# Transposing the global rows' probabilities of the last two batches by DMA instead of on TensorE

## The chip, the core and the metric

The kernel runs on one core of one Trainium2 chip. The metric is device microseconds (us) of one execution; lower is better. The kernel before took 308.22 us, the median of three runs that lie between 307.31 and 308.99.

## The reference

Block-sparse attention (4 batches, 8 heads, 768 positions, head size 64) is followed by a two-layer network on its output. Positions are grouped in 24 blocks of 32. A query block sees its neighbours, the first and the last block, and three sampled blocks. Queries of the first and the last block see all 768 keys; these are the *global rows* that the change is about.

```python
scores = scale * q @ k.T                       # per batch and head, 768 x 768
mask = (|blk_i - blk_j| <= 1) | blk_i in (0, 23) | blk_j in (0, 23) | sampled
attn = softmax(where(mask, scores, -1e9))      # over the keys
x = (attn @ v)                                 # -> 3072 tokens x 512
h = x @ w_in                                   # 512 -> 2048
out = (h * sigmoid(beta * h)) @ w_out          # 2048 -> 512, float32
```

## The kernel before

**Attention, ordinary rows.** Each batch has 11 *pairs* of query blocks, 44 in all, numbered n. For pair n, `kg` and `kn` on POOL (or DVE) collect its 8 key blocks per query block into KG, SP's DMAs `vg` fetch the value rows into VG (from pair 6 on three buffers in turn: a load for pair n waits for `av` of pair n - 3), `sc` on PE makes the scores, `mx` on DVE the row maxima, `ex` on ACT the exponentials PP, `rc` and `nrm` scale them, `tp` on PE transposes them, `ptv` on DVE or ACT moves the transposed tile to PT, `av` on PE multiplies with VG, and `xv` moves the result to xT. The sampled value rows are one DMA of 32 KB each, six for a pair, beside one or three larger ones; `vv` (L663) loads the block numbers of two pairs into SP's registers.

**Attention, global rows.** Each batch has four *units* w of 128 rows (4 heads x 32 queries) by 768 keys; over the batches they are numbered m = 0 to 15. `gs` (L911, PE) makes the scores of two units at once in four PSUM banks. Then for each unit: `gm` (L925, L927, DVE) the negated maximum; `ge` (L932, ACT) two exponentials of 384 columns into PG[m % 2]; `gr` (L939, L940, DVE) the reciprocal of the sum; `gn` (L943, POOL) scales PG; `gt` (L951, PE) six 128x128 transposes into one PSUM bank; `gptv` (L953, DVE) copies that bank into PTG. When all four units of a batch are in PTG, `gav` (L965, PE) multiplies with V and `gx` moves the result to xT. PG has two buffers, so `ge` of unit m waits for `gt` of unit m - 2. PTG has one, so `gptv` of a batch waits for `gav` of the batch before.

**The key order.** Key s stands in row p, step j of the value tile, with s = 6 p + j. So transpose j takes every sixth column of PG, from column j on.

**The network.** Tokens go through in eight groups G of 8 or 16 blocks: `h` (L1027, PE), `tanh` (L1033, ACT), `stt` (L1038, DVE), `y` (L1054, PE), `oe` (L316, ACT) and `od` (L1072 to L1075, SP's DMA to the output). A group needs the xT of its blocks; the last two groups, 6 and 7, hold batch 3 alone. The global blocks of a batch belong to its last group.

**Order.** Nothing is scheduled on the chip. A planner in the kernel (class `Plan`) runs a list scheduling in Python: every task has an engine or a choice of engines, a booked duration, a priority `prio` plus a hand-set `OFFSET`, its dependencies, and the PSUM banks that it opens and closes. DMA tasks on SP or ACT also carry `dma` (booked transfer time) and `hw` (DMAs that they issue). The planner's order of tasks is the order in which instructions are written; each engine then runs its own in that order and waits where a dependency is not met. Units of batch b carry the priorities `10.0 * ((5, 11.5, 18, 31)[b] + 0.5 * w) + 5`, where pair n carries 10 n.

Of the kernel before, what the change touches and what calls it, by code (L numbers as in the profile page):

```python
# [36 lines left out]
class Plan:  # L37
# [21 lines left out]
    def add(self, *a, **k):  # L59
        t = Task(*a, **k)  # L60
        self.tasks.append(t)
        return t
# [154 lines left out]
def kernel(  # L217
# [11 lines left out]
    nc = tc.nc  # L229

    B, H, S, D = q.shape
    BLK = 32
    NB = S // BLK
    P = 128
    J = S // P
# [24 lines left out]
    NLATE, PTA, ODS, AHEAD = 11, 1.0, 0.8, 3  # L260
    NHOT, NV = 0, 2
    NHL, UP = 4, 1024.0
    WIDE = 16

    SR, SG0, SN, SG1 = 0, 3, 4, 7
# [23 lines left out]
    PTG = sb("PTG", [P, J, 4, P])  # L289
# [14 lines left out]
    add = plan.add  # L304
    bank = lambda name: banks[plan.bank[name]]
# [26 lines left out]
    def emit_warm():  # L332
# [3 lines left out]
        out=warm[:, 0:1], in_=warm[:, 1:2], func=AF.Exp), deps=[t_warm0], prio=-150)  # L336
# [53 lines left out]
    for part, f in enumerate((emit_mask0, emit_mask1, emit_mask2)):  # L390
# [4 lines left out]
        deps=[t_mrow], prio=-90, lat=0.2, opens=("mask",))  # L395
    t_mask = add("maskc", "DVE", 0.2, lambda: nc.vector.tensor_copy(
        out=maskr[:, :, :].rearrange("x a b -> x (a b)"), in_=bank("mask")[:, 0:NM]),
        deps=[t_mb], prio=-66, closes=("mask",))
# [13 lines left out]
    pj = sb("pj", [P, J], FP32)  # L412
    mi32 = sb("mi32", [1, BLK], I32)

    def emit_selc():
# [8 lines left out]
        out=srow, in_=sf[:, 0:2 * NSEL, :].rearrange("o a r -> o (a r)")), deps=[t_idx], prio=-98)  # L424
    t_selw = []
    for f in range(2):
        def emit_sb(f=f):
# [9 lines left out]
            out=sel16[:, f * SH:(f + 1) * SH], in_=bank(("selb", f))[:, 0:SH]),  # L437
            deps=[tb], prio=-88, closes=(("selb", f),)))
    t_sel = [add(f"sel16.{j}", "DVE", 0.27, lambda j=j: nc.vector.tensor_scalar(
        out=sel[j], in0=sel16, scalar1=pj[:, j:j + 1], scalar2=None, op0=ALU.is_equal),  # L440
        deps=t_selw, prio=-66.2) for j in range(J)]
# [5 lines left out]
        out=beta_row, in_=moe_beta.rearrange("(q x) -> q x", q=FQ)), prio=-140, dma=0.1, hw=1)  # L447
    t_id32 = add("id32", "DVE", 0.2, lambda: nc.vector.tensor_copy(
        out=ident32, in_=identity[0:4, 0:4]), deps=[t_ident], prio=-64)

    def emit_betaT():
        for i in range(4):
# [3 lines left out]
                  deps=[t_beta0, t_id32], prio=-55, lat=0.2, opens=("beta",))  # L456
    t_beta = add("betah", "DVE", 0.2, lambda: nc.vector.tensor_scalar(
        out=beta_sb[:, :].rearrange("x (q i) -> x i q", i=4),
        in0=bank("beta")[:, 0:N_FFC].rearrange("x (i q) -> x i q", i=4),
        scalar1=0.5, scalar2=None, op0=ALU.mult),  # L460
        deps=[t_betaT], prio=-55, closes=("beta",))
# [20 lines left out]
    for z, (i, nm, t, dst) in enumerate(((2, "V", v, None), (0, "K", k, RK), (1, "Q", q, RQ))):  # L482
        for f in range(2):
            tl = add(f"ld{nm}0.{f}", "SP", 0.47, lambda i=i, t=t, f=f: nc.sync.dma_start(
                out=stage_half(i, f) if i < 2 else v_stage[:, f * HH:(f + 1) * HH, :],
                in_=src6(t, 0, f * HH, HH)), prio=-80 + z * 2 + f, dma=2.0 if z + f else 3.4, hw=1)
# [4 lines left out]
            for hp in range(2 * f, 2 * f + 2):  # L491
# [3 lines left out]
                        out=dst[:, 2 * hp:2 * hp + 2, :], in_=stage32(i, hp)),  # L495
                    deps=[tl], prio=-72 + 4 * i + hp)
# [3 lines left out]
        out=(w_in_sb[0:1, 0, 0:1], w_in_sb[0:1, 0, 2 * FQ * P:2 * FQ * P + 1], w_out_sb[0:1, 0, 0:1])[i],  # L500
        in_=vgate(n)), prio=-57.5 + i, deps=[ld0["Q", 1]] if n < 0 else [])
# [8 lines left out]
    for fq in range(4):  # L510
        fs = slice(fq * FQ * P, (fq + 1) * FQ * P)
        for c in range(0, 4, 2):
            t_win.append(add(f"win{fq}.{c // 2}", "POOL", 0.6, lambda c=c, fs=fs: nc.gpsimd.dma_start(
                out=w_in_sb[:, c:c + 2, fs], in_=w_in_r[:, c:c + 2, fs]),
                deps=[touch[fq // 2]], prio=-50 + 0.2 * fq + 0.05 * c, dma=1.3, bulk=THR))
    for c in range(4):
        for f in range(2):
            ps = slice(64 * f, 64 * f + 64)
            t_wout.append(add(f"wout{c}.{f}", "POOL", 0.6, lambda c=c, ps=ps: nc.gpsimd.dma_start(
                out=w_out_sb[ps, 4 * c:4 * c + 4, :].rearrange("x i m -> x (i m)"), in_=w_out_r[c, ps, :]),  # L520
                deps=[touch[2]], prio=-49 + 0.2 * c + 0.1 * f, dma=1.3, bulk=THR))
# [7 lines left out]
    for b in range(B):  # L529
        pr = prep_prio(b)  # L530
# [369 lines left out]
    for b in range(B):  # L900
        for w, (blk, u) in enumerate((bl, u) for bl in (NB - 1, 0) for u in range(2)):
            pr = 10.0 * ((5, 11.5, 18, 31)[b] + 0.5 * w) + 5
            m, s_ = gun, SG[gun % 2]
            pg = PG[gun % 2]

            def emit_gs(b=b, blk=blk, m=m):
                for hf in range(2):
                    for hp in range(NHP):
                        for uu in range(2):
                            rows = slice(uu * D, (uu + 1) * D)  # L910
                            nc.tensor.matmul(  # L911
                                bank(("GS", m + uu, hf))[hp * BLK:(hp + 1) * BLK, 0:S // 2],
                                lhsT=QT[b % 2][rows, hp, blk * BLK:(blk + 1) * BLK],
                                rhs=KT[b % 2][rows, hp, hf * (S // 2):(hf + 1) * (S // 2)],
                                start=True, stop=True, skip_group_check=True,
                                tile_position=(uu * D, hp * BLK))
            if u == 0:
                gs = add(f"gs{m}", "PE", 0.34, emit_gs, deps=([mx[GSB + w, 1]] if b == 0 else []) + [evK[b, hp] for hp in range(NHP)] +
                         [evQ[b, hp] for hp in range(NHP)], prio=pr, lat=0.2,
                         opens=tuple(("GS", m + uu, hf) for uu in range(2) for hf in range(2)))  # L920
                gsc_all.setdefault(b, []).append(gs)

            def emit_gm(m=m, s_=s_):
                for hf in range(2):
                    nc.vector.tensor_reduce(out=s_[:, hf:hf + 1], in_=bank(("GS", m, hf))[:, 0:S // 2],  # L925
                                            axis=AX.X, op=ALU.max, negate=True)
                nc.vector.tensor_reduce(out=s_[:, 2:3], in_=s_[:, 0:2], axis=AX.X, op=ALU.min)  # L927
            gm = add(f"gm{m}", "DVE", 1.15, emit_gm, deps=[gs] + ([gn[m - 2]] if m >= 2 else []), prio=pr)

            def emit_ge(m=m, s_=s_, pg=pg):  # L930
                for hf in range(2):
                    nc.scalar.activation(  # L932
                        out=pg[:, hf * (S // 2):(hf + 1) * (S // 2)], in_=bank(("GS", m, hf))[:, 0:S // 2],
                        func=AF.Exp, bias=s_[:, 2:3], scale=1.0, accum_out=s_[:, 3 + hf:4 + hf])
            ge = add(f"ge{m}", "ACT", 1.12, emit_ge, deps=[gm] + ([gt[m - 2]] if m >= 2 else []), prio=pr,
                     closes=(("GS", m, 0), ("GS", m, 1)))

            def emit_gr(s_=s_):
                nc.vector.tensor_reduce(out=s_[:, 5:6], in_=s_[:, 3:5], axis=AX.X, op=ALU.add)  # L939
                nc.vector.reciprocal(out=s_[:, 6:7], in_=s_[:, 5:6])  # L940
            gr = add(f"gr{m}", "DVE", 0.26, emit_gr, deps=[ge], prio=pr)
            gn[m] = add(f"gn{m}", {"POOL": 0.9, "DVE": 0.44}, None, lambda eng, s_=s_, pg=pg: (
                nc.vector if eng == "DVE" else nc.gpsimd).tensor_scalar(  # L943
                out=pg, in0=pg, scalar1=s_[:, 6:7], scalar2=1.0, op0=ALU.mult, op1=ALU.mult),
                deps=[gr], prio=pr)

            def emit_gt(m=m, pg=pg):
                o = bank16(("GT", m))
                pj = pg[:, :].rearrange("x (p j) -> x j p", j=J)
                for j in range(J):  # L950
                    nc.tensor.transpose(out=o[:, j * P:(j + 1) * P], in_=pj[:, j, :], identity=identity)  # L951
            gt[m] = add(f"gt{m}", "PE", 0.34, emit_gt, deps=[gn[m]], prio=pr, lat=0.2, opens=(("GT", m),))
            gptv[m] = add(f"gptv{m}", "DVE", 0.47, lambda m=m, w=w: nc.vector.tensor_copy(  # L953
                out=PTG[:, :, w, :],
                in_=bank16(("GT", m))[:, 0:J * P].rearrange("x (j m) -> x j m", j=J)),
                deps=[gt[m]] + ([gavt[b - 1]] if b else []), prio=pr, closes=(("GT", m),))
            gun += 1

        def emit_gav(b=b):
            o = bank(("GO", b))  # L960
            for hp in range(NHP):
                for j in range(J):
                    for u in range(2):

                        nc.tensor.matmul(  # L965
                            o[u * D:(u + 1) * D, hp * 2 * BLK:(hp + 1) * 2 * BLK],
                            lhsT=Vn[b % 2][:, j, (2 * hp + u) * D:(2 * hp + u + 1) * D],
                            rhs=PTG[:, j, u::2, hp * BLK:(hp + 1) * BLK],
                            start=(hp + j == 0), stop=(j == J - 1), skip_group_check=True,
                            tile_position=(0, u * D))  # L970
        gavt[b] = add(f"gav{b}", "PE", 0.75, emit_gav, deps=[gptv[gun - 4 + w] for w in range(4)] +
                      vperm[b], prio=pr, lat=0.2, opens=(("GO", b),))
        def emit_gx(eng, b=b):
            c0 = x_of(b * NB + NB - 1)
            copy_on(eng, xT[:, :, c0:c0 + 2 * BLK],
                    bank(("GO", b))[:, 0:2 * NHP * BLK].rearrange("x (h m) -> x h m", h=NHP))
        evs = [add(f"gx{b}", {"DVE": 0.42, "ACT": 0.38}, None, emit_gx, deps=[gavt[b]], prio=pr,
                   closes=(("GO", b),))]
        for blk in (0, NB - 1):
            xw[b * NB + blk] = evs  # L980
# [133 lines left out]
```

## Time and profile before

| | |
|---|---|
| median of three runs | 308.22 us |
| the profiled execution, its own time | 306.66 us |
| its span, first to last instruction | 304.9 us |
| granted TensorE clock, mean | 0.994 |
| L951 `gt`, 96 transposes on PE | 216 / 219 / 260 ns each (min, median, max) |
| L953 `gptv`, 16 copies on DVE | 536 / 548 / 557 ns each |
| L932 `ge`, 32 exponentials on ACT | 569 / 580 / 630 ns each |
| L943 `gn`, 16 scalings on POOL | 894 / 902 / 904 ns each |
| `gav` of batches 0, 1, 2, 3 starts at | 78.5, 107.8, 160.2, 215.0 us |
| last `av` (pair 43) starts at | 263.9 us |

All times in a trace are us from the start of the span. A matmul's duration overlaps with that of the next one, so PE's work is read from how far the starts lie apart, not from the sum of durations. The execution's own time is 1.8 us longer than its span. "SPq" is SP's queue of DMA issues, which the page does not count as busy time. Loads of K, Q and V of the next batch run on POOL's own DMA queue.

### The profile page before, as it was taken

To read this page: it belongs to the slowest core of one execution; us is meant where nothing else is said; L and a number is where in the kernel's file an instruction comes from. 1 tells how busy PE (TensorE), PEld (TensorE's weight loads), DVE (VectorE), ACT (ScalarE), POOL (GpSimd) and SP (SyncE) were. 2 spreads that over 40 slices of the span, in tenths; PEclk is the share of its full clock that TensorE was granted. 3 is DMA by queue.
4 is the path that set the end of the run, shared out by engine and by line. 5 is a ranking of instruction groups with operands and counts; after the bars stand their busy time and mean duration, and the time that the engine had idled before them with its cause. 6 is when DMAs were issued, how large, how long until landed. Compare 5 with 4: busy or idle time off the path is not lost.

```text
span 304.9 us, 11891 instructions
## 1 busy us (share of the span) xinstructions
PE 284.7 (93%) x4209; PEld 177.3 (58%) x4209; DVE 241.3 (79%) x562; ACT 219.8 (72%) x639; POOL 172.9 (57%) x513
## 2 busy tenths in 40 slices
PE   2699869999999899999998999999999999999994
PEld 0455658657855785665556555556555555554671
DVE  4857989999999999999999579989789765780260
ACT  3347669889788999898759599978689837771461
POOL 3079895044689678899784486868646942100000
PEclk9999979999999999999999999999999999999999
DMA  7999999978999462479943633234343242101202
GB/s 254 370 295 207 233 208 231 221 219 136 165 208 183 119 190 74 123 145 166 210 124 116 203 123 97 73 85 124 100 155 106 75 121 90 37 0 57 83 1 69
DMA packets 43445, 44.17 MB, mean 145 GB/s; under 512 B 6005, under 2 KB 39414, under 8 KB 43386
## 3 DMA queue, kind: packets, MB, share of 16 engines
q1 hardware_dynamic: 31056, 32.13, 35.1%
q0 software_dynamic: 12320, 11.27, 24.8%
q8 instruction: 33, 0.54, 0.7%
q14 instruction: 26, 0.21, 0.2%
q10 hardware_dynamic: 10, 0.01, 0.0%
HBM read 45.23 MB, written 9.44 MB: 179 GB/s over the span
## 4 chain that ended last, share of the span: by engine, by line
PE 70%; DVE 18%; DMA 6%; issue 2%; ACT 2%; SPq 1%; POOL 0%; DVEq 0%
PE bank L1027 26%; PE bank L1054 20%; PE bank L821 5%; DMA VG<-VT 4%; DVE ST L776 4%; PE bank L848 4%; PE bank L560 3%; PE bank L729 3%; DVE SG L925 3%; DVE VG L312 3%; DMA g<-in_k_dram 3%; PE bank L753 2%; PE bank L763 2%; PE bank L856 2%; DVE PTG L953 2%
## 5 line engine op out<-in xcount | busy, mean ns | idle before, releaser
L784 ACT ACTIVATE PP<-bank,ST 128x256 f16<-128x256 f32 x176 | 81.4, 479 | 20.6 <-DVE ST L776 12.4
L1027 PE MATMUL bank<-xT,w_in_sb 128*128 128x256 f16 (+1 forms) x512 | 94.0, 328 | 1.4 <-DVE g L1038 0.9
L1054 PE MATMUL bank<-w_out_sb,g 128*128 128x512 f16 x384 | 92.3, 380 | 0.0
L1038 DVE SCALAR_TENSOR_TENSOR g<-t,bank 128x512 f16<-128x512 f16 (+1 forms) x128 | 66.5, 546 | 19.4 <-ACT t L1033 19.0
L1033 ACT ACTIVATE t<-bank,beta_sb 128x512 f16<-128x512 f32 (+1 forms) x128 | 70.4, 594 | 13.5 <-PE bank L1027 9.6
L807 POOL TENSOR_SCALAR PP<-PP,ST 128x256 f16<-128x256 f16 x132 | 63.4, 497 | 27.6 <-DVE ST L801 27.6
L634 POOL COPY KG<-KT 128x64 f32 x264 | 52.0, 247 | 32.4 <-PE bank L763 18.8
L1027 PEld LDWEIGHTS <-w_in_sb 128*128 128x128 f16 x512 | 53.7, 115 | 25.8 <-issue 4.6
L776 DVE TENSOR_REDUCE ST<-bank 128x2 f32<-128x512 f32 x88 | 57.4, 680 | 3.4 <-PE bank L763 2.1
L1054 PEld LDWEIGHTS <-g 128*128 128x128 f16 x384 | 34.4, 98 | 38.2 <-issue 4.9
L784 ACT ACTIVATION_READ_ACCUMULATOR PP<-bank,ST 128x1 f32 x176 | 37.0, 210 | 0.0
L316 ACT ACTIVATE osb<-bank 128x512 f32<-128x512 f32 x24 | 14.5, 605 | 19.6 <-PE bank L1054 19.5
L312 DVE COPY PT<-bank 128x1024 f16<-128x1024 f16 x39 | 26.7, 685 | 2.4 <-PE bank L821 1.6
L821 PE MATMUL bank<-identity,PP 128*128 128x128 f16 x352 | 28.0, 224 | 0.3 <-ACT PP L784 0.3
L943 POOL TENSOR_SCALAR PG<-PG,SG 128x768 f16<-128x768 f16 x16 | 14.4, 900 | 23.9 <-ACT PG L932 19.8
L821 PEld LDWEIGHTS <-PP 128*128 128x128 f16 x352 | 22.8, 100 | 7.6 <-issue 1.3
L312 DVE CAST xT<-bank 64x256 f16<-64x256 f32 (+1 forms) x33 | 13.9, 420 | 8.4 <-ACT xT L310 7.4
L848 PEld LDWEIGHTS <-VG 128*128 128x128 f16 x448 | 16.5, 98 | 6.7 <-DMA VG<-VT 1.0
L932 ACT ACTIVATE PG<-bank,SG 128x384 f16<-128x384 f32 x32 | 18.3, 585 | 2.4 <-DVE SG L927 2.2
L312 POOL COPY KG<-KT 128x384 f32<-128x384 f32 (+3 forms) x47 | 19.6, 438 | 0.4 <-PE bank L763 0.4
L763 PE MATMUL bank<-KG,QT 64*32 64x256 f16 x704 | 18.0, 269 | 1.1 <-issue 1.1
L848 PE MATMUL bank<-PT,VG 128*128 128x64 f16 x448 | 17.7, 193 | 0.1
(107 smaller groups left out, 309.8 us busy)
## 6 DMA issues: line engine op xcount, KB each, us to landing
VG<-VT SPq DMA_DIRECT2D x220, 32.0 KB, 2.6
VG<-VT SPq DMA_DIRECT2D x32, 192.0 KB, 2.6
out_dram<-osb SPq DMA_DIRECT2D x20, 256.0 KB, 2.4
RV<-in_v_dram POOLq DMA_DIRECT2D x6, 384.0 KB, 6.4
RK<-in_k_dram POOLq DMA_DIRECT2D x6, 384.0 KB, 8.3
VT<-Vn SPq DMA_DIRECT2D x3, 768.0 KB, 3.9
RQ<-in_q_dram POOLq DMA_DIRECT2D x6, 384.0 KB, 6.4
w_in_sb<-in_moe_w_in_dram POOLq DMA_DIRECT2D x8, 256.0 KB, 8.0
```

Of the source, the lines that this page charges most:

```text
L312: (nc.vector if eng == "DVE" else nc.gpsimd).tensor_copy(out=out, in_=in_)
L634: nc.gpsimd.tensor_copy(out=kg32[:, g, :, (SR + r) * W:(SR + r + 1) * W], in_=kt32[:, :, bass.ds(vals[3 * g + r], W)])
L763: nc.tensor.matmul(bk[u][hp * BLK:(hp + 1) * BLK, g * 256:(g + 1) * 256], lhsT=QT[b % 2][u * D:(u + 1) * D, hp, (i0 + g) * BLK:(i0 + g + 1 ...
L776: mx[n, u] = add(f"mx{n}.{u}", "DVE", 0.6, lambda n=n, u=u, sb_=sb_: nc.vector.tensor_reduce(out=sb_[:, 0, 2 * u:2 * u + 2], in_=bank(("S" ...
L784: nc.scalar.activation(out=pb[:, u, g, :], in_=bank(("S", n, u))[:, g * 256:(g + 1) * 256], func=AF.Exp, bias=sb_[:, 0, 2 * u + g:2 * u + ...
L807: (nc.vector if eng == "DVE" else nc.gpsimd).tensor_scalar(out=pb[:, u, g, :], in0=pb[:, u, g, :], scalar1=sb_[:, 2, 2 * u + g:2 * u + g + ...
L821: nc.tensor.transpose(out=o[:, s * P:(s + 1) * P], in_=pb[:, u, g, c * P:(c + 1) * P], identity=identity)
L848: nc.tensor.matmul(o[:, (g * NHP + hp) * 2 * BLK:(g * NHP + hp + 1) * 2 * BLK], lhsT=vgb[:, g, c, hp * P:(hp + 1) * P], rhs=pt[:, g, c, :, ...
L1027: nc.tensor.matmul(o[:, 0:TW], lhsT=w_in_v[:, c, f // 4, f % 4, :], rhs=xT[:, c, c0:c0 + TW], start=(c == 0), stop=(c == NHP - 1))
L1033: lambda G=G, f=f, TW=TW, tt=tt: nc.scalar.activation(out=tt[:, 0:TW], in_=bank(("H", G, f))[:, 0:TW], func=AF.Tanh, bias=0.0, scale=beta_ ...
L1038: lambda G=G, f=f, TW=TW, tt=tt, gg=gg: nc.vector.scalar_tensor_tensor(out=gg[:, f, 0:TW], in0=tt[:, 0:TW], scalar=1.0, in1=bank(("H", G, ...
L1054: nc.tensor.matmul(o[:, :], lhsT=gg[:, f, s * P:(s + 1) * P], rhs=w_out_sb[:, f, :], start=(f == 0), stop=(f == N_FFC - 1))
```

## The change

For all four batches the exponentials of a unit are written to PG in the order (j, p) instead of (p, j): ACT reads its 384 PSUM columns with a step of six and writes six runs of 64 columns. `gt` then reads 128 neighbouring columns for each j instead of every sixth.

For batches 2 and 3 (`GD = 2`, units 8 to 15) `gt` and `gptv` are replaced by one DMA, `gtd`, which SP issues with `transpose=True`, from PG straight into PTG (128 x 768, 2 bytes, 192 KB). It waits for `gn` of its unit and for `gav` of the batch before. `ge` of unit m + 2 waits for its landing, and so does `gav`. The planner books 1.25 us of SP and 0.3 us of transfer for it. The table `OFFSET` has no entry for `gtd`.

```diff
+    GD = 2
@@ emit_ge
-                        out=pg[:, hf * (S // 2):(hf + 1) * (S // 2)], in_=bank(("GS", m, hf))[:, 0:S // 2],
+                        out=pg[:, :].rearrange("x (j p) -> x j p", j=J)[:, :, hf * hw_:(hf + 1) * hw_],
+                        in_=bank(("GS", m, hf))[:, 0:S // 2].rearrange("x (p j) -> x j p", j=J),
@@ emit_gt
-                pj = pg[:, :].rearrange("x (p j) -> x j p", j=J)
+                pj = pg[:, :].rearrange("x (j p) -> x j p", j=J)
...
+            if b >= GD:
+                gt[m] = gptv[m] = add(f"gtd{m}", "SP", 1.25, lambda m=m, w=w, pg=pg: nc.sync.dma_start(
+                    out=PTG[:, :, w, :], in_=pg[:, :], transpose=True),
+                    deps=[gn[m]] + ([gavt[b - 1]] if b else []), prio=pr, dma=0.3, hw=1)
+                gun += 1
+                continue
```

(`hw_` is 64, half of the 128 columns of one j.)

More of the change, by code (lines that the diff above doesn't have):

```diff
@@ L931, in emit_ge @@
                 for hf in range(2):
+                    hw_ = P // 2
                     nc.scalar.activation(
-                        out=pg[:, hf * (S // 2):(hf + 1) * (S // 2)], in_=bank(("GS", m, hf))[:, 0:S // 2],
+                        out=pg[:, :].rearrange("x (j p) -> x j p", j=J)[:, :, hf * hw_:(hf + 1) * hw_],
+                        in_=bank(("GS", m, hf))[:, 0:S // 2].rearrange("x (p j) -> x j p", j=J),
                         func=AF.Exp, bias=s_[:, 2:3], scale=1.0, accum_out=s_[:, 3 + hf:4 + hf])
```

## The prediction

> **What bounds the kernel now.** I read first the busy time of each engine by stretches of the span, cut where the last two batches' units lie (columns: stretch, its length, then each engine's busy time).
>
> ```profile
> core 0: us, PE busy (x) PEld busy (x) DVE busy (x) ACT busy (x) POOL busy (x), PEclk, DMA share, GB/s
> 120.00:149.00 29.00, 28.81 (x409) 16.90 (x407) 28.41 (x67) 25.38 (x81) 26.41 (x71) 1.00 0.78 153
> 149.00:163.00 14.00, 13.18 (x221) 7.64 (x219) 13.53 (x29) 8.67 (x28) 8.86 (x25) 1.00 0.57 129
> 163.00:199.00 36.00, 36.00 (x514) 21.60 (x513) 29.62 (x56) 30.20 (x87) 24.12 (x82) 1.00 0.41 122
> 199.00:216.50 17.50, 17.01 (x283) 9.52 (x280) 16.26 (x42) 12.37 (x39) 12.06 (x28) 1.00 0.41 118
> 216.50:264.00 47.50, 47.50 (x581) 26.98 (x580) 34.79 (x68) 35.44 (x107) 26.76 (x82) 1.00 0.33 99
> ```
>
> From 120 to 264 PE idles only 0.19 + 0.82 + 0.49 = 1.5 us, at a granted clock of 1.00. Work taken off PE there brings the end forward by its own length, and any new wait of PE puts the end back by its length. DVE is nearly full where the units run (13.53 of 14.00, 16.26 of 17.50) and has air elsewhere.
>
> The page's busy times leave SP's queue out, so next the timeline of SP alone, and the landings from the list of DMA issues:
>
> ```profile
> 178.37 28.08 SPq L714 DMA_DIRECT2D VG<-VT  x45
> 206.54 0.37 SPq L1072 DMA_DIRECT2D out_dram<-osb  x1
> ...
> VG<-VT SPq DMA_DIRECT2D x32, 192.0 KB, 2.6
> out_dram<-osb SPq DMA_DIRECT2D x20, 256.0 KB, 2.4
> ```
>
> 45 value loads in 28.08 us are 0.62 us each. In the trace's single instructions a sampled load takes 0.50 (0.18 of register work, 0.32 of issue), and `vv` 0.75; the rest is single issues of 1.0 to 1.5 us, one in some 9 us. From 163 to 221 SP is never idle for over 0.4 us: it is as full as PE. Value rows land shortly before use: those of pairs 26, 28 and 29 at 169.55, 181.69 and 185.69, while their `av` start at 171.9, 184.0 and 188.0, 2.3 us later each. Pairs 33 and 34 have 6.3 and 9.7 us.
>
> Last the timeline of batch 3's units, engine by engine:
>
> ```profile
> 203.76 0.90 POOL L943 TENSOR_SCALAR PG<-PG,SG 128x768 f16<-128x768 f16 x1
> 206.16 0.83 PE L951 MATMUL bank<-identity,PG 128*128 128x128 f16 x12
> 207.04 0.58 ACT L932 ACTIVATE PG<-bank,SG 128x384 f16<-128x384 f32 x1
> 208.02 1.01 DVE L953 COPY PTG<-bank 128x768 f16<-128x768 f16 x2
> 210.60 1.01 ACT L310 COPY PT<-bank 128x1024 f16<-128x1024 f16 x1 [1.14 <-PE bank L821]
> 212.12 0.63 PE L848 MATMUL bank<-PT,VG 128*128 128x64 f16 x16
> ```
>
> Unit 12 is scaled by 204.66. `gt` of units 12 and 13 is over by 206.99, and ACT starts unit 14 (`ge14`) at 207.04, just after PG is free. ACT then makes `ptv33` (210.60), which PE's `av33` (212.12) needs.
>
> **The change part by part.** The sum is made against the profiled execution's own 306.66 us, which lies 1.56 below the median of 308.22; the difference found is put on the median.
>
> *Transposes off PE.* The twelve transposes at 206.16 hold PE until the next matmul at 206.83: 0.67 us, 0.335 a unit. Eight units: 2.7 us, all on the path: **-2.7**.
>
> *Copies off DVE.* 1.01 us for two, 0.5 a unit, 4 us in all. DVE ends no wait of PE from 163 to 199; around batch 3's units PE's whole idle is 0.49. I book **0**, at best -0.5.
>
> *The exponentials' new pattern, 32 instructions.* The trace has none with a step of six. ACT's nearest strided read is KT<-bank: 826 ns for 768 elements (1.08 ns each), against 1015 for 1024 read in a row (0.99). At 8% of 580 ns it adds 0.05 us each, 1.5 us over all; below that it could be nothing. Half lie in batches 0 and 1, where from 80 to 108 DVE is busy 26.46 of 28 us and ACT 24.45, and ACT has 5 us to spare from 199 to 216.5: **0**; without that cover, up to +1.5. The contiguous weight loads of the remaining 48 transposes (125 ns now; 100 for `tp`, which reads in a row) lie under matmuls 0.055 apart: 0.
>
> *What `gtd` costs SP and the DMA.* No transposing DMA is in the trace. On SP an issue costs from 0.37 (an output DMA) to 1.66 (the longest single value load); the diff books 1.25, and I take that, nearer to the long end because one instruction has six 128x128 blocks to hand out. To landing: 192 KB took 2.6 and 256 KB 2.4 after issue, the slowest value loads (around 142, beside POOL's loads) 6.0 to 6.5. I take 2.5 plus the 0.9 by which it is issued longer than a value load: 3.4.
>
> *Batch 2.* SP gets 4 x 1.25 = 5.0 us more. To know who stands beside whom I use the planner's booked starts for the kernel before, for order alone: `gn10` ends at 146.9 booked, 154.70 in the trace (7.8 later); the value load booked at that moment (pair 24's second) is issued at 152.60, 5.5 later. So SP comes to `gtd10` some 2 us before its data and waits with pair 24's and 25's loads behind it. Of the 7 us, SP's waits for outputs at 160 to 163 (2.5) and for earlier landings from 136 to 147 (the 2.5 of units 8 and 9) take 5.0. 2.1 stay, on loads with 2.3 us of slack, of which PE's own gain in this batch (1.4) leaves 0.9. Pair 26 or 28 waits for 1.2: **+1.2**.
>
> *Batch 3.* SP gets 5.0 us more again, where loads are 6 to 10 us ahead: 0 there. But `ge14` now waits for unit 12's DMA instead of `gt`. The planner books the end of `gn12` at 195.7 and `vv35` on SP from 195.8 to 196.7, so `gtd12` stands about behind `vv35`. In the trace `gn12` ends at 204.66 (9.0 later), but `vv35` at 209.90 (13.2 later): POOL's task and SP's, booked for one moment, are 4 to 5 us apart. The batch 2 transposes shift SP alike in plan and run, so I leave this lag. `gtd12` is issued at 210.0 and lands at 213.4. ACT stands at `ge14` from 207.04 on, 6.4 us, with `ge15`, `ptv33` and the exponentials of pair 34 behind it; DVE stands at `gr14`. `ge14` and `ge15` take 2.2 as now, `ptv33` one more: `av33` starts at 217.0 instead of 212.12, while PE, rid of `gt12` and `gt13`, is there at 211.4: 5.6 us. The planner sees part of it: it books `gtd12` to land at 199.6 and so moves `ge14` from 197.8 to some 199.8, and 2.0 us of other PE work moves ahead of `av33`. **+3.6**. Ends: 0, if SP comes to `gtd12` right behind `gn12`; 5.6 without that cover. `gav3` gets later too; only the last group's `h`, at 287, needs it: 0.
>
> *Sum:* -2.7 + 1.2 + 3.6 = +2.1 us: 308.8 by the profiled execution, 310.3 on the median.
>
> *A page against the change.* The Trainium skill's "VectorE: DVE Perf Modes", section "The three transpose paths", gives 1309 ns for 128x128 by DMA and 390 by TensorE. Here six TensorE blocks run in 0.335 us, so pipelined they are far cheaper than the page's single one. Six DMA blocks strung together would by that page be 7.9 us, and with 7.9 in place of 3.4 the sum above would be +6.6; an estimate. The same skill's "Advanced Engine Details and Errata", section "X-Bar Transpose (TRN2)", says the contrary, that such DMAs are as fast as ordinary ones. No run here shows either yet.
>
> **The rivals.**
>
> *Faster: the wait at `ge14` doesn't come.* If SP's order puts `gtd12` and `gtd13` ahead of two pairs' loads, which the slack of pairs 33 and 34 allows, they land by 208.1 and ACT loses about 1 us, inside its idle time (1.14 before `ptv33`). This is decided where SP reaches `gtd12` before about 205.5. Then -2.7 + 1.2, or -2.7 if batch 2's loads hold as well: -1.6 to -2.7, 305.5 to 306.6 on the median. For it: SP's booked tasks there are loads not needed for 6 us. Against it: SP runs its program in order, and its lag on POOL in the trace.
>
> *No change.* The wait is shorter (2 to 3 us, SP having caught up in 199 to 210), and gain and wait cancel within 1.5 us: 306.7 to 309.7.
>
> *Much slower: the transposes land late.* If one takes 6.5 us, like the slowest value loads, `ge14` and `ge15` are 3.1 us later than in the sum, and SP's later loads, which reuse the eight landing semaphores in turn, wait for them: +5 to +8, 313 to 316. The page's 7.9 above belongs to this case. For it: six blocks in one DMA. Against it: the DMA engines are busy a share of 0.41 there and 192 KB lands in 2.6.
>
> *It does not relieve PE.* If PE waits elsewhere by as much as it saves, busy time falls by 2.7 and nothing else changes; this is part of "no change".
>
> **How the numbers follow.** About 0.5%, 1.54 us, is what a measurement of this kernel can tell from no change. The forecast, slower by 1.6 to 4 us (309.8 to 312.2), gets 0.43; faster 0.24; no change 0.22; much slower 0.11. The planner also lays out all later work anew, which can move the end by a microsecond or two either way; this is why no case gets more. So faster 0.24, same 0.22, slower 0.54. The range cuts the best end of "faster" and the worst of "much slower": 305.8 to 314.5.
>
> **What would show it.** Right: PE's L951 rows fall from 96 to 48; a wait of ACT at L932 for a DMA into PTG, over 3 us, around 205 to 215; PE idle 3 to 4 us there instead of 0.49; SP's issues of the transpose 1 to 1.5 us each and landings of 3 to 4. Wrong: `ge14` starting within 1.5 us of unit 13's exponentials ending as now, a landing over 6, value loads named before `av` in batch 2 for more than 2 us, or PE idle unchanged and the end 2.7 earlier.

## Result and profile after

After the change the kernel takes 313.11 us (median of 4 runs, 311.93 to 313.63) against 308.29 before (307.31 to 308.99): 4.8 us more, a ratio of 1.0153 [1.0111, 1.0196]. The profiled execution of after took 313.63 us (span 311.9), the slowest of its four; that of before, 306.66 (304.9), was the fastest of its own. So the traces lie 7.0 apart and the medians 4.8. In what follows medians hold all runs of a kernel; the ratios leave disturbed runs out, and can differ from the quotient of the medians by up to half a per cent.

Line numbers of after are one to ten higher than before's (`ge` L935, `gn` L947, `gt` L955, `gtd` L957, `gav` L975, `av` L849, the value loads L715). First the rows of the changed parts, from the trace's answers by line and by tile (durations in ns as min/median/max, then the first and last start):

```profile
L955 PE MATMUL bank<-identity,PG x48: 216/219/230, 66.7 to 106.6; 128*128 128x128 f16 x48
L935 ACT ACTIVATE PG<-bank,SG x32: 571/582/630, 62.9 to 218.5; 128x384 f16<-128x384 f32 x32
L957 SPq DMA_TRANSPOSE PTG<-PG x8: 1210/1234/2299, 128.7 to 222.2; - x8
...
DMA to landing us min/median/max: 2.7/3.6/6.4
```

TensorE has 48 transposes left of 96. The strided exponentials take 582 ns against 580 before. One transposing DMA holds SyncE's queue for 1.23 us and lands 3.6 us after its issue.

Then the same stretches of the span as before, for TensorE's column:

```profile
core 0: us, PE busy (x) PEld busy (x) DVE busy (x) ACT busy (x) POOL busy (x), PEclk, DMA share, GB/s
120.00:149.00 29.00, 27.60 (x402) 15.53 (x387) 27.34 (x67) 25.11 (x80) 26.51 (x79) 1.00 0.75 139
149.00:163.00 14.00, 13.90 (x171) 7.33 (x170) 11.84 (x27) 11.13 (x30) 11.12 (x28) 1.00 0.96 168
163.00:199.00 36.00, 33.26 (x506) 20.32 (x505) 26.02 (x50) 28.46 (x82) 20.60 (x66) 1.00 0.47 136
199.00:216.50 17.50, 16.48 (x226) 8.48 (x225) 14.86 (x35) 9.85 (x31) 13.25 (x37) 1.00 0.37 100
216.50:264.00 47.50, 45.12 (x621) 25.61 (x621) 34.59 (x70) 36.18 (x113) 27.67 (x80) 1.00 0.43 117
```

TensorE now idles 1.40, 0.10, 2.74, 1.02 and 2.38 us in them, 7.6 us where before it was 1.5. What it stood for is in the list of TensorE's waits from 105 to 272 us (in total, times, longest), of after:

```profile
PE bank L849 <- DMA VG<-VT: 3.4, 3, 1.7
PE bank L1064 <- ACT PG L935: 1.7, 1, 1.7
PE bank L975 <- DMA PTG<-PG: 1.2, 2, 0.7
PE bank L849 <- DVE PT L313: 0.7, 1, 0.7
```

and of before:

```profile
PE bank L965 <- DVE PTG L953: 1.3, 3, 0.8
```

So the largest new wait is not at batch 3's transposes at all: 3.4 us go to the gathered value rows, at 140.19 (1.27), 177.18 (0.47) and 183.28 (1.68). The wait at L1064 (215.69, 1.66) is for the PSUM bank that `ge14` empties, the one behind it (218.38, 0.68) for `ptv33`, and 1.2 us are `gav2` and `gav3` standing for their own transposes. The value rows that TensorE lacks at 140.19 come with a load that SyncE issued at 136.79, behind `gtd8` and `gtd9`, and that landed at 141.33, just after `gtd9` (140.59). In before's trace the same load was issued at 130.69 and landed at 132.27. So it was issued 6.1 us later and then took 4.5 us to land instead of 1.6.

What ScalarE and SyncE did at those places, first ScalarE's timeline at `ge14`, then SyncE's at the same time and in batch 2 (start, length, instruction; idle before it in brackets):

```profile
210.92 0.60 ACT L317 ACTIVATE osb<-bank 128x512 f32<-128x512 f32 x1 [0.30 <-PE bank L1064]
216.63 0.58 ACT L935 ACTIVATE PG<-bank,SG 128x384 f16<-128x384 f32 x1 [5.12 <-DMA PTG<-PG]
```

```profile
211.07 1.80 SPq L715 DMA_DIRECT2D VG<-VT  x4
212.96 3.36 SPq L957 DMA_TRANSPOSE PTG<-PG  x2
216.51 0.43 SPq L715 DMA_DIRECT2D VG<-VT  x1
```

```profile
153.87 1.35 SPq L715 DMA_DIRECT2D VG<-VT  x3
158.35 1.27 SPq L957 DMA_TRANSPOSE PTG<-PG  x1
159.72 1.31 SPq L715 DMA_DIRECT2D VG<-VT  x1
161.14 1.21 SPq L957 DMA_TRANSPOSE PTG<-PG  x1
```

GpSimd ended `gn12` at 209.20; SyncE issued value loads until 212.9 and came to `gtd12` at 212.96, 3.8 us late. It landed at 216.52, and ScalarE had stood for 5.12 us. In batch 2 it is the other way round: SyncE had nothing left ahead of `gtd10` at 156.1 and stood 2.3 us for its data, with the next value loads behind it. The last load ahead of `gtd10` is issued 4.0 us later than in before's trace, the loads behind `gtd11` 10 us later.

Laid event by event, after's trace lags before's by 1.3 us from 56 us on, before anything of the change acts: between 30 and 45 us the granted clock was 0.69 of full speed there, and 0.91 in before's trace. At the exponentials of pair 33 (204 us) the lag is 4.5, at the end 7.0. Batch 2's stretch thus cost 3.2 us net of what it saved, batch 3's 2.5.

### The profile page after: what moved, and what is told of

Same layout as the page of the kernel before. It is cut to its first block, busy times and chain, and to the rows that moved or that the text cites. A ratio compares the mean times of both kernels' runs of the same rounds, so it can differ in the third digit from the quotient of the medians.

```text
span 311.9 us, 11801 instructions
## 1 busy us (share of the span) xinstructions
PE 286.3 (92%) x4161; PEld 176.9 (57%) x4161; DVE 235.7 (76%) x555; ACT 222.6 (71%) x639; POOL 173.9 (56%) x512
## 4 chain that ended last, share of the span: by engine, by line
PE 59%; DMA 14%; DVE 12%; issue 4%; SPq 3%; ACT 3%; POOL 2%; POOLq 1%; DVEq 0%; ACTq 0%
PE bank L1037 19%; PE bank L1064 17%; DMA VG<-VT 8%; PE bank L822 5%; PE bank L849 3%; DVE ST L777 3%; PE bank L561 3%; DMA PTG<-PG 3%; PE bank L730 3%; SPq L715 3%; DMA g<-in_k_dram 3%; PE bank L857 2%; PE bank L764 2%; DVE SG L926 2%; DVE PT L313 2%
## 5 line engine op out<-in xcount | busy, mean ns | idle before, releaser
L1064 PE MATMUL bank<-w_out_sb,g 128*128 128x512 f16 x384 | 91.9, 380 | 1.8 <-ACT PG L935 1.7
L1064 PEld LDWEIGHTS <-g 128*128 128x128 f16 x384 | 34.7, 98 | 41.1 <-issue 6.8
L947 POOL TENSOR_SCALAR PG<-PG,SG 128x768 f16<-128x768 f16 x16 | 14.9, 932 | 27.0 <-ACT PG L935 22.5
L313 DVE COPY PT<-bank 128x1024 f16<-128x1024 f16 x36 | 24.7, 686 | 4.6 <-PE bank L822 4.2
L313 DVE CAST xT<-bank 64x256 f16<-64x256 f32 (+1 forms) x36 | 15.1, 419 | 12.6 <-PE bank L849 6.1
L849 PEld LDWEIGHTS <-VG 128*128 128x128 f16 x448 | 16.8, 98 | 11.1 <-issue 5.6
L935 ACT ACTIVATE PG<-bank,SG 128x384 f16<-128x384 f32 x32 | 18.3, 586 | 6.3 <-DMA PTG<-PG 5.1
L849 PE MATMUL bank<-PT,VG 128*128 128x64 f16 x448 | 18.6, 193 | 4.5 <-DMA VG<-VT 3.4
```

The lines of the kernel that those rows point to most:

```text
L313: (nc.vector if eng == "DVE" else nc.gpsimd).tensor_copy(out=out, in_=in_)
L849: nc.tensor.matmul(o[:, (g * NHP + hp) * 2 * BLK:(g * NHP + hp + 1) * 2 * BLK], lhsT=vgb[:, g, c, hp * P:(hp + 1) * P], rhs=pt[:, g, c, :, ...
L1064: nc.tensor.matmul(o[:, :], lhsT=gg[:, f, s * P:(s + 1) * P], rhs=w_out_sb[:, f, :], start=(f == 0), stop=(f == N_FFC - 1))
```

## Experiments

Each kernel ran beside the kernel before on the same chip. The first four shared a chip and a median of before of 307.75, the next four 307.60, the next three 307.74, the last 307.47.

**1. The stride alone.** All transposes on TensorE, only the exponentials' stores and the transposes' reads as in the change; the order of instructions is that of before.

```diff
-            if b >= GD:
+            if b >= B:
```

> The exponentials' column stride for all batches, but every unit transposed on TensorE and copied by DVE as before; the order of instructions on every engine is that of the kernel before. If the cost of the change sits in SP's queue and the waits behind it: within 1 us of before, ACT's 32 exponentials at 580 to 590 ns as before. If the strided exponentials cost: at least 1.5 us slower and L935 rows over 600 ns.

308.14 us, ratio 1.0008 [0.9983, 1.0034]. The stored column stride costs nothing that can be measured. Its trace, too, runs a constant 1.1 us behind before's from 46 us on: the early lag belongs to the execution, not to the change.

**2 and 3. One batch alone.**

```diff
-            if b >= GD:
+            if b == 3:      # experiment 2;   b == 2 in experiment 3
```

> DMA transposes for batch 3 only; everything up to unit 12 stands in the order of the kernel before. If the wait of unit 14's exponentials for unit 12's DMA costs what the trace after suggests (its lag grows by 2.5 us there, gain on PE included): +2 to +3 us against before, with ACT idle 4 to 6 us before L935. If nearly all the loss lies with batch 2's value loads: -1.4 to 0 us.

> DMA transposes for batch 2 only. If the waits of PE for value loads after SP has stood at unit 10's transpose cost what the trace after suggests (3.5 us of PE idle between 140 and 190, less 1.4 of PE work): +2 to +2.5 us against before. By the prediction's own term for batch 2 (+1.2 - 1.4): within 0.5 us of before.

Batch 3 alone: 313.17 us, 1.0147 [1.0102, 1.0192]. Batch 2 alone: 312.78, 1.0137 [1.0083, 1.0192]. By the medians each alone costs as much as both together; both expectations were too low. TensorE's waits from 105 to 272 us, of batch 3 alone:

```profile
PE bank L975 <- DMA PTG<-PG: 2.9, 1, 2.9
PE bank L1064 <- ACT PG L935: 2.9, 1, 2.9
```

and of batch 2 alone:

```profile
PE bank L849 <- DMA VG<-VT: 3.8, 4, 1.1
PE bank L975 <- DMA PTG<-PG: 0.5, 1, 0.5
```

Batch 3 has two waits of TensorE, not one: that behind `ge14` and, 9 us later, `gav3` standing 2.9 us for the DMA. Batch 2 has value rows. Where both are on, batch 3's waits are shorter (3.0 us instead of 5.8): SyncE comes to `gtd12` at nearly the same time (212.96 against 212.2), while TensorE, held up in batch 2, comes to them 2 us later. One loss covers part of the other.

The waits are not all of it. In the traces of experiments 2, 3, 4 and 8, but not in after's, the granted clock falls once more behind 60 us. Two stretches of after, then one of experiment 3 and one of experiment 2 (columns: stretch, its length, TensorE's busy time, granted clock, DMA share, GB/s):

```profile
150.00:200.00 50.00, 47.15 (x703) 1.00 0.59 141
200.00:250.00 50.00, 46.60 (x622) 1.00 0.41 112
...
150.00:200.00 50.00, 46.45 (x659) 0.97 0.59 138
200.00:250.00 50.00, 44.01 (x589) 0.97 0.49 114
```

Looked at more finely, the clock is at half from 189.1 to 192.5 us in experiment 3 and from 228.2 to 231.7 in experiment 2, each time within 0.4 us of the end of a wait of TensorE (188.81 and 228.04). What that costs can be read from experiment 3, since up to the exponentials of pair 33 its TensorE, VectorE, ScalarE and SyncE have the same instructions in the same order as in the change. From the exponentials of pair 13 to these the change takes 112.9 us and experiment 3 takes 114.6, with TensorE idle for 6.1 us in both. The difference, 1.7 us, is half of the 3.4 at half clock. So in this trace batch 2 alone loses what it loses in the change, 3.2 us, and the clock the rest. Whether a wait brings the clock down was not tested; none followed the wait of 2.9 us at 213.60 in experiment 2. For executions without a trace there is only the mean clock: 0.971 to 0.986 in the four of experiment 2, 0.978 to 0.994 (median 0.989) in the thirteen of before beside them.

**4. Four probability buffers.** With both batches by DMA, unit 14 no longer reuses unit 12's buffer.

```diff
-    PG = [sb(f"PG{i}", [P, S]) for i in range(2)]
+    PG = [sb(f"PG{i}", [P, S]) for i in range(3)]
-            pg = PG[gun % 2]
+            pg = (PG + [sel16])[gun % 4]
-            ge ... deps=[gm] + ([gt[m - 2]] if m >= 2 else []),
+            ge ... deps=[gm] + ([gt[m - (4 if b >= GD else 2)]] if m >= 2 else []),
```

> The changed kernel with four PG buffers for batches 2 and 3 (a third one and a tile that is free by then), so that unit m's exponentials wait for unit m - 4's transpose, long landed. If the wait at unit 14 is a cost of its own: 2 to 3 us faster than the changed kernel (+2 to +3 against before), no idle of ACT before L935 over 1 us in batch 3. If that wait only covers another one (value loads, PSUM banks): as slow as the changed kernel, +4 to +5.

312.88 us, 1.0151 [1.0109, 1.0193]: as slow as the change. ScalarE's wait at `ge14` is gone from the trace, and TensorE's waits read

```profile
PE bank L849 <- DMA VG<-VT: 3.5, 3, 1.4
PE bank L849 <- DVE g L1048: 1.4, 1, 1.4
PE bank L849 <- issue: 0.5, 1, 0.5
```

In this trace batch 3's stretch costs nothing any more: the lag against before is 6.6 us at pair 33 and 6.5 at the end. So the wait at `ge14`, and what followed from it, was a cost of its own in the change. Batch 2's stretch costs 5.0 us here instead of 3.2; 1.7 of that go with a clock at half from 189.6 to 193.0. The median, as slow as the change, shows neither.

**5. No transposing at all.** The upper bound of what the removal brings.

```diff
-                gt[m] = gptv[m] = add(f"gtd{m}", "SP", 1.25, ...)
+                gt[m] = gptv[m] = gn[m]
```

> The change with its eight DMAs taken out and nothing in their place: the eight transposes of batches 2 and 3 on TensorE and the eight copies on VectorE are gone, SyncE has none of the new work; the value products of these two batches read what batch 1 left (the transposing of batches 2 and 3 is left out). This is the most that the removal can bring. Theory 1 (the removal is worth its 2.7 us, and the loss of the change is all in the DMAs and their waits): 305.0 to 306.2. Theory 2 (TensorE's 48 transposes lie in gaps that other waits make, the removal is worth less than 0.7 us): 307.4 to 308.5.

303.32 us, 0.9857 [0.9824, 0.9890]: 4.3 us faster than before, more than the 2.7 booked. TensorE is busy 2.5 us less (282.2 against 284.7), and its idle time from 105 to 272 us falls from 1.5 to 0.3: before's 1.3 us at `gav` for VectorE's copies into PTG, shown above, goes too. So the change gave up this gain and 4.8 us more: its DMAs and what stands for them cost some 9 us.

**6. Plain copies in place of the transposing DMAs**, every engine's order as in the change.

```diff
-                    out=PTG[:, :, w, :], in_=pg[:, :], transpose=True),
+                    out=PTG[:, :, w, :], in_=pg[:, :].rearrange("x (j p) -> x j p", j=J)),
```

> The kernel after, every engine's order the same, with the eight DMAs as plain copies of the same 192 KB to the same place (the transposing is left out). Theory 1 (what costs is the place in SyncE's order: it comes late to a DMA whose data has long been there, or stands for data with value loads behind it): hold falls from 1.23 us to some 0.4 to 0.8 and the rest stays: 311 to 313, with ScalarE's wait at the third group of batch 3 at 3.5 to 5 us. Theory 2 (the DMA's own hold and landing): 308 to 309.5, that wait under 2.5 us.

310.79 us, 1.0105 [1.0068, 1.0142]. From the trace's answer by tile:

```profile
L957 SPq DMA_DIRECT2D PTG<-PG x8: 594/610/1181, 128.2 to 219.0; - x8
...
  ACT PG L935: 4.7, 1
...
DMA to landing us min/median/max: 2.6/2.8/5.2
```

The hold halves (0.61) and the landing is 0.8 us earlier, yet ScalarE stands at `ge14` for 4.65 us instead of 5.12, and TensorE still stands 2.2 us for value rows. Most of the loss is the place in SyncE's order, as theory 1 says, though the time lies just under its range; the transposing itself accounts for some 2 us, with intervals that overlap.

**7. The same DMAs from ScalarE's queue.**

```diff
-                gt[m] = gptv[m] = add(f"gtd{m}", "SP", 1.25, ... nc.sync.dma_start(
+                gt[m] = gptv[m] = add(f"gtd{m}", "ACT", 1.25, ... nc.scalar.dma_start(
```

> The eight transposing DMAs from ScalarE's queue in place of SyncE's. Value loads on SyncE are then free of them. Theory 1 (place in SyncE's order): the value loads come as before the change, but ScalarE, which has little to spare, stands at each DMA until the product on GpSimd is done: 309 to 312, the waits in the profile move from matmuls that want value rows to those that want ScalarE. Theory 2 (the DMA's own hold and landing, whatever the queue): 312 to 314 with the wait at the third group of batch 3 as in the change.

307.85 us, 1.0017 [0.9992, 1.0041]: no different from before, better than either theory said. ScalarE's timeline around units 12 to 14:

```profile
207.30 1.23 ACTq L957 DMA_TRANSPOSE PTG<-PG  x1
208.62 1.25 ACTq L957 DMA_TRANSPOSE PTG<-PG  x1
...
210.90 0.58 ACT L935 ACTIVATE PG<-bank,SG 128x384 f16<-128x384 f32 x1 [0.32 <-DMA PTG<-PG]
```

`gn12` ended at 207.0, and the DMA was issued 0.3 us later instead of 3.8; `ge14` waits 0.32 us. The hold is the same from either queue and ScalarE has room for it. The gain is spent elsewhere: TensorE waits 1.3 us for value rows, 1.0 for xT and 0.4 for each of two things on VectorE, all of them before 163 us. By the lag, batch 2's stretch loses 1.3 us against before and batch 3's gains 1.6.

**8 and 9. Batch 3 alone, its two waits taken away one after the other.** Experiment 8 is batch 3 alone with four buffers and with each DMA placed 6 us after its data is due; in experiment 9 `gav3` is placed 14 us later as well.

```diff
                     deps=[gn[m]] + ([gavt[b - 1]] if b else []), prio=pr,
+                    slack=6,                          # 8 and 9
         gavt[b] = add(f"gav{b}", "PE", 0.75, emit_gav, ...
+                      slack=14 if b == 3 else 0,      # 9 alone
```

> Batch 3 alone by DMA, four probability buffers instead of two (so the third group doesn't wait for the first one's DMA), and the planner told to place each DMA 6 us after its data is due, which also puts the last product of probabilities and values 8 us later in TensorE's order. Theory 1 (the waits in the orders are what costs, the DMA itself is cheap): the waits at the third group and at the last product are gone, half of the removal's gain is left: 306.5 to 307.5. Theory 2 (the DMAs delay SyncE's other work wherever they stand): 309 to 312, with TensorE's waits on value loads behind 210 us.

> Batch 3 alone by DMA from SyncE, four probability buffers, each DMA placed 6 us after its data is due, and now the last product of probabilities and values placed 14 us later again in TensorE's order (only the last feed-forward group needs it). Where TensorE stood 4.4 us at that product with the DMAs 6 us late, it should not stand now. Theory 1 (all that batch 3 loses is TensorE standing in its own order for what the DMA has not yet brought): 305.8 to 307.0, no TensorE wait of over 0.3 us between 200 and 260 us. Theory 2 (SyncE's 5 us of issuing delay its other transfers enough to eat the gain): 307.5 to 309.5, with waits on value rows behind 215 us.

Experiment 8: 312.33 us, 1.0101 [1.0061, 1.0142]; one of its ten runs took 308.03, the rest 311.2 to 314.5. The profiled one is the slowest, with the clock at half from 227.9 to 234.8 us, so its waits need not be those of the others. Experiment 9: 306.54 us, 0.9957 [0.9933, 0.9981]. TensorE's waits in the two, of 8 (`sel` is the tile that serves as the fourth buffer):

```profile
PE bank L975 <- DMA PTG<-PG: 3.2, 1, 3.2
PE bank L975 <- DMA PTG<-sel: 1.2, 1, 1.2
```

and all that there is of 9:

```profile
PE bank L975 <- DVE PTG L963: 0.8, 1, 0.8
```

Without the wait at `ge14`, but with DMAs 6 us later, `gav3` took it all over; with `gav3` later too, batch 3's DMAs are a gain of 1.2 us on the medians. In the trace of 9 the lag against before falls from 2.4 us at pair 33 to 1.0 at the end: 1.4, which is batch 3's half of the 2.7 booked. SyncE's four holds cost TensorE no wait here, as the prediction had it for loads that run 6 to 10 us ahead. This version beats both kernels. What the four buffers and the late `gav3` would bring without the DMAs was not run.

**10 and 12. The same mends with batch 2.** Experiment 10 has both batches, experiment 12 batch 2 alone; four buffers, DMAs 6 us and last products 10 us later.

```diff
         gavt[b] = add(f"gav{b}", "PE", 0.75, emit_gav, ...
+                      slack=10 if b >= 2 else 0,      # 10;   b == 2 in 12
```

> Both batches by DMA from SyncE as in the change, with four probability buffers, each DMA placed 6 us after its data is due (so that SyncE should not come to it before the product on GpSimd is done), and both batches' last products placed 10 us later. Theory 1 (only standing in order costs; with SyncE never standing for data and TensorE never for the transposed probabilities the removal's gain shows): 304.5 to 306.5. Theory 2 (in batch 2 the DMAs' 5 us of holding SyncE delay the value loads behind them, wherever the DMAs stand): 308 to 310, with TensorE's waits on value rows at 135 to 190 us of 2 us or more in all.

> Batch 2 alone by DMA from SyncE with the mends that made batch 3 alone a gain: four probability buffers, each DMA placed 6 us after its data is due, the last product of the batch 10 us later. Against batch 2 alone without them (312.78). Theory 1 (standing in the orders is all that costs): 305.8 to 307.0, as for batch 3. Theory 2 (in batch 2 SyncE is so full of value loads that its 5 us of holding come out as late value rows wherever the DMAs stand): 308.5 to 311, with TensorE's waits on value rows at 135 to 190 us of 1.5 us or more.

Both: 308.91 us, 1.0016 [0.9984, 1.0048]. Batch 2 alone: 308.84, 1.0039 [1.0007, 1.0071], against 312.78 without the mends. The trace of 10 is of a run of 307.24, below its median, and has 0.8 us of waits for value rows, 0.35 of them between 135 and 190 us: the median lies in theory 2's range, but the 2 us of waits that it names are not in this trace. The waits of 12:

```profile
PE bank L849 <- DMA VG<-VT: 1.7, 2, 1.0
PE bank L822 <- ACT PG L935: 1.2, 1, 1.2
PE bank L849 <- ACT t L1043: 0.6, 1, 0.6
```

In 12 SyncE no longer stands at `gtd10`: it issues loads without a pause of over 0.4 us from 150.71 to 186.87, and the DMA at 160.55. Its pauses of over 0.35 us between 128 and 200 us are 2.9 us in all (before 6.1, after 5.0). TensorE still waits 1.7 us for value rows, 1.0 at 186.96 and 0.7 at 206.65. A queue without pauses can't take up a hold, so theory 2 is the likely one for this batch, and its time came true; of the waits that it names only the first lies in its window. The mends removed 3.9 of the 5.0 us of the median, not the loss; part of that may be the half clock of experiment 3's trace, which the trace of 12 doesn't have. In 12 batch 3 too has four buffers, with its transposes on TensorE, and its stretch loses 0.6 us.

**11. ScalarE's queue with four buffers and late last products.**

```diff
-                gt[m] = gptv[m] = add(f"gtd{m}", "SP", 1.25, ... nc.sync.dma_start(
+                gt[m] = gptv[m] = add(f"gtd{m}", "ACT", 1.25, ... nc.scalar.dma_start(
-            pg = PG[gun % 2]
+            pg = (PG + [sel16])[gun % 4]
+                      slack=10 if b >= 2 else 0,      # gav
```

> Both batches by DMA from ScalarE's queue, four probability buffers, both batches' last products placed 10 us later. Against the same from ScalarE without the two mends (307.85): theory 1 (TensorE's time is what counts, ScalarE's 10 us of issuing lie in its idle third): 304.5 to 306.5. Theory 2 (ScalarE standing at its DMAs delays its exponentials and evictions, which TensorE waits for): 307 to 309, with waits on ScalarE's xT and PG in place of the value rows.

308.95 us, 1.0037 [1.0014, 1.0061]. It does not help: TensorE waits 1.28 us behind ScalarE's exponentials (155.56), 0.98 for xT (162.86) and 1.13 at 216.97 for a batch-3 pair's sums on VectorE. Moving the DMAs between queues moves the wait.

## Why the prediction was right, and where its sum was not

The direction (slower), the range and the cause (ordered queues that put SyncE in the wrong place at the wrong time) held; the size was +2.1 forecast and +4.8 measured. The 313.1 lies above the band that the prediction held likeliest (309.8 to 312.2) and in that of the rival "much slower", though not for that rival's reason. Of its four signs against itself two were seen: value rows late by more than 2 us in batch 2, and a landing over 6 us.

- *Transposes off PE, -2.7*: 2.5 us less of busy TensorE in experiment 5, and batch 3's half of it, 1.4, realised in experiment 9. Right.
- *Copies off DVE, 0, at best -0.5*: mis-sized. TensorE's 1.3 us at `gav` hung on these copies, and experiment 5 got 4.3 in all. The prediction looked for such waits from 163 us on; 0.8 of the 1.3 us lie at 160.45, in the stretch where its own table has 0.82 us of idle.
- *The stride, 0*: right (experiment 1).
- *Hold 1.25, landing 3.4*: 1.23 and 3.6. Right. The Trainium skill's "VectorE: DVE Perf Modes", section "The three transpose paths", would by its single-block figure have given an estimate of 7.9 for six blocks. The whole of six blocks lands in 2.7 to 2.8 us where the queue is free (experiment 9: 2.7 to 2.9), so that figure must not be multiplied by the blocks of one DMA. The Trainium skill's "Advanced Engine Details and Errata", section "X-Bar Transpose (TRN2)", holds them as fast as ordinary DMAs: against the plain copy of experiment 6 landing took 3.6 instead of 2.8 and the hold was twice as long, so it holds nearly for the transfer and not for the issue.
- *Batch 2, +1.2*: the term that failed. SyncE's standing at `gtd10` was foreseen (2.3 against "some 2 us"), but not that its pauses would hide so little. The prediction let 5.0 of the 7 us vanish in SyncE's waits for outputs and earlier landings. Of before's 6.1 us of pauses between 128 and 200 us, after still has 2.7 beside those 2.3: only 3.4 was cover. For units 8 and 9 it let SyncE's waits for earlier landings take up both DMAs, but the first late row, at 140.19, is theirs (1.27 us). TensorE stood for value rows 3.4 us instead of 1.2, plus 0.5 at `gav2`. By the lag, batch 2 came to +3.2 net, where the sum had 1.2 less 1.35.
- *Batch 3, +3.6*: right in size, less so in shape. The mechanism is as told: SyncE reaches `gtd12` late behind value loads (3.8 us, 5.3 forecast) and `ge14` stands (5.1, 6.4 forecast). The lag says +2.5 net of 1.35 saved. Experiments 4 and 7 show that the wait goes with another buffer, or with a queue that is at the place in time, and that batch 3's loss goes with it. But TensorE's first wait came a little ahead of `av33`, at a matmul that wanted the bank `ge14` empties.
- *"`gav3` gets later: 0"*: wrong. Only the last group needs its result, but TensorE runs its own order, and everything behind `gav3` waits with it: 0.7 us in the change, 2.9 in experiment 2, 4.4 in experiment 8. This is what experiment 9 took away to turn the loss into a gain.
- *"Any new wait of PE puts the end back by its length"*: too little for the traces of experiments 2, 3, 4 and 8, where a clock at half costs more on top of the waits; in the change's own trace nothing of the kind is seen behind 46 us.
- *The rivals*: "much slower" by late landings did not decide the result. The one landing of 6.35 us, `gtd9` in batch 2, kept no reader of PTG waiting, but the value rows that TensorE lacked at 140.19 landed right behind it; how much of that wait is the landing and how much the late issue is not separated. "Faster" is what experiment 9 shows for batch 3, by moving the waiters rather than the DMAs ahead.

What stays open: what brings the clock down in experiments 2, 3, 4 and 8, and how much of their loss it is in the executions without a trace; that batch 3's waits are shorter when TensorE comes later is argued from the traces, not tested by a run of its own; and the 1.2 us of experiment 12 that stand behind ScalarE's exponentials were not taken apart, since the planner orders much of the other work anew.

## What to carry to other kernels

Here work moved from a compute engine to a DMA cost its queue's order before it cost bandwidth: ask when the in-order queue reaches the instruction, against when its data is ready. If early, everything behind it waits; if late, everyone who needs it or its buffer does. Then place the consumers as well: a product that nobody needs for 50 us still blocks an in-order engine if it stands in its program too early. And look at the granted clock of every trace, stretch by stretch, before a loss is put down to waits: here two traces with the same instructions and the same idle time were 1.7 us apart by it. Count a queue's pauses as cover only where the new work can really slide into them, and move work only in stages where the queue runs ahead (batch 3 here, not batch 2).

## What was not expected of the hardware

A DMA of 192 KB that transposes six 128x128 blocks holds its queue 1.23 us from SyncE and 1.24 from ScalarE, a plain copy to the same place 0.61, a value load of 32 KB 0.32. The granted clock between 30 and 45 us differs from run to run of nearly the same work, 0.91, 0.69 and 0.68 in the profiled runs of before, after and experiment 9, and shifts all that follows by 1 to 2 us; two traces are better compared by the growth of the lag behind that place than by their ends. Late in the program the clock stayed full in the trace of the change, and was at half for 3.4 us in those of experiments 2, 3 and 4 and for 6.9 us in that of experiment 8.
